# Attention with a gated MLP on one core: four score banks that also hold the maxima's first-block scores and the values' output

## Chip, core and metric

The kernel runs on one core of a Trainium2 chip. The metric is device time in microseconds (us), the median of three runs: 740.32 us before the change (739.99 to 740.38). The profiled execution, from which all durations are taken, took 740.08 us.

## What is computed

The input x has 2048 tokens of 512 channels. It is normalized; one branch is attention with 32 heads of 16 channels in which each token sees itself and the 255 tokens before it, the other is an MLP with 1792 hidden channels whose result, through SiLU, gates the first.

```
xn = layernorm(x)
q, k, v = heads of (xn @ wqkv)                       # 32 heads x 16
scores = q k^T / 4, kept where 0 <= i - j < 256
s = (softmax(scores) @ v) @ wo
g = silu(gelu(layernorm(xn) @ w1 + b1) @ w2 + b2)
out = x + s * g
```

All is float32. The matmuls work on pairs of rounded parts: each operand is split into a high part and the rest, and three products (high x high, high x rest, rest x high) are summed.

## The kernel before

**The slots.** Attention runs over 8 groups of four heads (n) and 16 blocks of 128 keys (kb); one slot t = 16 n + kb handles one key block of one group. A loop (line 834) writes the slots' instructions out in order, and the class Ordered (line 27) keeps each engine to the order in which the code names them, so the order on TensorE is that of this loop. Within a slot stand, in order:

1. `prob_block(.., 1)` (line 555): the scores of head pair 1. Two matmuls (one for each head, in the two halves of the array's rows) give 128 keys x up to 384 queries into two PSUM banks; ScalarE takes the exponential of both into SBUF (tile pt), and GpSimd sets to zero what lies outside the window.
2. `max_block` (line 503) for the query block 12 slots ahead (LEAD): four matmuls give the scores of that block against its own and the preceding key block in xy (two banks). VectorE copies into the masked places the scores against the first key block of the window (`first_scores`, line 494; four matmuls into zo), by a predicated copy, and reduces the maxima over keys. These maxima go back into the operands later, so that the exponentials need no further subtraction. Query blocks 0 and 1 of a group have no first block and take a constant.
3. `fill_in(t, 0)`: a share of other work for TensorE, cut into small units: projections of later groups, later the values' projection and MLP products. `tandem` (line 440) spreads two such jobs over several slots, with a high half and a low half of the contraction in the two halves of the array's rows, into the two banks fb; its function `places` (line 449) says how many units go to the first half of a slot and how many to the second. When a tandem ends (slot t1) both banks are copied out, by ScalarE in most of them.
4. `prob_block(.., 0)`: the scores of head pair 0.
5. `fill_in(t, 1)`: the second share of other work.
6. `first_scores` for the next slot's query block, both pairs.
7. `pv_step` (line 577): the values of the slot before: for up to three key blocks and four heads a matmul of 17 x 128 into otb, four of them side by side in the array's columns. ScalarE (VectorE in the slots where a tandem has just ended) copies otb to oraw.

**Where these lie in PSUM.** There are eight banks of 512 columns. xy has two. zo has two: columns 0 to 256 of both hold the first-block scores, columns 256 to 384 of the second hold the values' output otb (line 195). fb has two, for fills. The last two are a pool of single banks (ps_st) before slot 0, for transposes and the first values' projections, and from slot 0 on the tile stb, the scores of a pair; both pairs of a slot use it in turn. In the last 12 slots, which have no maxima left, pair 1 uses xy instead.

**After the slots** comes the MLP with the gated output, in another set of PSUM tiles. The change does not touch it.

## Time and profile before

| | before |
|---|---|
| median of runs | 740.32 us |
| profiled execution | 740.08 us |
| its span | 738.4 us |
| TensorE busy | 725.1 us (98%) |
| VectorE busy | 509.8 us (69%) |
| ScalarE busy | 444.0 us (60%) |
| GpSimd busy | 297.6 us (40%) |
| granted TensorE clock, mean | 0.999 |

How to read the profile: the span runs from the first to the last instruction. PE is the matmuls of TensorE, PEld its weight loads, DVE is VectorE, ACT ScalarE, POOL GpSimd, SP the engine that issues DMAs. Matmuls are pipelined and their ends are modelled, so neighbouring rows can overlap a little. In the timeline a row is a run of like instructions: start, length, engine, line, operation, output <- inputs, shapes, count, and in brackets the idle time before it with what ended it. In the groups by shape the columns are the group and its count, then busy time and mean ns of one, then the idle time ahead of them, by what ended it. All instructions carry line 43, that of the helper that issues them, so groups are told apart by the names of tiles: pt<-stb is an exponential, stb<-qk the scores of a pair, xy<-qk the maxima's scores, zo<-qk the first-block scores, zo<-pt,vt the values, fb fills, oraw<-zo the copy of the values' output, xy<-upper,zo the predicated copy.

### The profile page before, as it was taken

How to read it: one execution, taken by the hardware profiler on the slowest of the kernel's cores; microseconds unless marked ns; L12 is line 12 of the kernel's file. 1: busy time of each engine (PE TensorE's matmuls, PEld its weight loads, DVE VectorE, ACT ScalarE, POOL GpSimd, SP SyncE). 2: the span in 40 equal slices, each digit the busy share in tenths (PEclk: the TensorE clock that was granted, in tenths of full speed). 3: DMA queues.
4: the chain of work that ended last, by engine and by line, in shares of the span. 5: the costliest groups of instructions: out<-in, count | busy, mean ns of one | idle time of the engine just before them, and what ended most of it. 6: DMA issues, size and time to landing. Idle time of an engine off the chain costs nothing.

```text
span 738.4 us, 18757 instructions
## 1 busy us (share of the span) xinstructions
PE 725.1 (98%) x7360; PEld 587.2 (80%) x7360; DVE 509.8 (69%) x790; ACT 444.0 (60%) x744; POOL 297.6 (40%) x644
## 2 busy tenths in 40 slices
PE   8999999999999999999999999999999999999997
PEld 7886777777778888777776688888888888888886
DVE  7886677877766678887772577656667855667733
ACT  7757767877777676778877756443644734541001
POOL 7413757867666555767867600120102000001102
PEclk9999999999999999999999999999999999999999
DMA  8633356766555524747724397657452322163711
GB/s 292 194 69 77 83 144 165 198 162 186 146 145 148 158 66 153 177 127 184 206 84 148 106 323 194 178 134 206 108 110 100 111 76 86 60 183 118 228 40 57
DMA packets 84697, 105.71 MB, mean 143 GB/s; under 512 B 37312, under 2 KB 37568, under 8 KB 84608
## 3 DMA queue, kind: packets, MB, share of 16 engines
q1 hardware_dynamic: 84608, 104.51, 50.7%
q8 instruction: 58, 0.95, 0.5%
q14 instruction: 31, 0.25, 0.1%
HBM read 54.53 MB, written 32.77 MB: 118 GB/s over the span
## 4 chain that ended last, share of the span: by engine, by line
PE 91%; ACT 4%; DVE 2%; POOL 1%; DMA 1%; issue 1%; SPq 0%; DVEq 0%; ACTq 0%
PE acc L43 21%; PE fb L43 19%; PE zo L43 13%; PE stb L43 9%; PE p L43 9%; PE s L43 6%; PE h L43 6%; PE xy L43 5%; ACT pt L43 4%; PE pv L43 3%; POOL pt L43 1%; DVE xy L43 1%; DMA x<-in_x_dram 1%; DVE mt L43 0%; PE tr L43 0%
## 5 line engine op out<-in xcount | busy, mean ns | idle before, releaser
L43 POOL TENSOR_SCALAR_AFFINE_SELECT pt<-pt 128x256 f32<-128x256 f32 x480 | 193.0, 426 | 128.9 <-ACT pt L43 126.1
L43 ACT ACTIVATE pt<-stb 128x768 f32<-128x768 f32 (+1 forms) x244 | 188.7, 773 | 52.6 <-PE stb L43 46.3
L43 DVE TENSOR_REDUCE mt<-xy 128x4 f32<-128x1024 f32 (+1 forms) x128 | 152.6, 1192 | 4.4
L43 DVE COPY_PREDICATED xy<-upper,zo 128x512 f32<-128x512 int32 x112 | 77.8, 694 | 70.4 <-PE xy L43 63.0
L43 POOL TENSOR_TENSOR xo<-xo,gated 128x512 f32<-128x512 f32 x15 | 19.9, 1328 | 235.0 <-DVE gated L43 195.6
L43 PE MATMUL fb<-xnT,wqb 64*128 64x512 f32 (+1 forms) x684 | 104.6, 397 | 0.0
L43 PE MATMUL zo<-pt,vt 128*17 128x128 f32 x2880 | 103.7, 275 | 0.3 <-POOL pt L43 0.3
L43 PE MATMUL stb<-qk 64*128 64x384 f32 (+1 forms) x488 | 94.6, 383 | 6.0 <-ACT pt L43 4.3
L43 PE MATMUL acc<-w,gh 128*128 128x512 f32 x320 | 98.4, 389 | 0.0
L43 PEld LDWEIGHTS stb<-qk 64*128 64x128 f32 x488 | 45.8, 183 | 48.3 <-ACT pt L43 41.4
L43 PEld LDWEIGHTS zo<-pt,vt 128*17 128x17 f32 x2880 | 67.5, 97 | 15.6 <-issue 5.0
L43 PEld LDWEIGHTS fb<-xnT,wqb 64*128 64x128 f32 (+1 forms) x684 | 64.8, 185 | 9.5 <-issue 0.6
L43 PEld LDWEIGHTS acc<-w,gh 128*128 128x128 f32 x320 | 60.1, 188 | 12.4
L43 PE MATMUL acc<-w,gl 128*128 128x512 f32 x160 | 62.2, 389 | 0.0
L43 PE MATMUL xy<-qk 64*128 64x256 f32 (+2 forms) x536 | 58.3, 291 | 0.2 <-DVE mt L43 0.2
L43 PEld LDWEIGHTS xy<-qk 64*128 64x128 f32 x536 | 46.6, 185 | 6.8 <-issue 3.2
L43 ACT COPY oraw<-zo 128x128 f32<-128x128 f32 x108 | 28.7, 266 | 30.8 <-PE zo L43 20.4
L43 ACT ACTIVATE gated<-acc 128x512 f32<-128x512 f32 x16 | 8.7, 595 | 59.3 <-DVE acc L43 59.3
L43 PE MATMUL s<-wos,ohl 128*128 128x512 f32 (+1 forms) x204 | 44.3, 376 | 0.0
L43 PEld LDWEIGHTS s<-wos,ohl 128*128 128x128 f32 x204 | 36.8, 188 | 7.1
L43 ACT COPY p<-p 128x512 f32<-128x512 f32 x21 | 12.3, 585 | 48.6 <-PE p L43 41.4
L43 PEld LDWEIGHTS zo<-qk 64*128 64x128 f32 x448 | 37.5, 185 | 4.8 <-DVE xy L43 1.8
(190 smaller groups left out, 1238.9 us busy)
## 6 DMA issues: line engine op xcount, KB each, us to landing
qk<-sh SPq DMA_DIRECT2D x128, 128.0 KB
qk<-pjr SPq DMA_DIRECT2D x64, 128.0 KB
oT_d<-oraw SPq DMA_DIRECT2D x32, 256.0 KB
w_d<-in_w_dram SPq DMA_DIRECT2D x14, 512.0 KB
x<-in_x_dram SPq DMA_DIRECT2D x16, 256.0 KB
or<-oT_d SPq DMA_DIRECT2D x16, 256.0 KB
w<-rden_d SPq DMA_DIRECT2D x16, 256.0 KB
xo<-in_x_dram SPq DMA_DIRECT2D x16, 256.0 KB
```

What stands on the lines that cost most here:

```text
L43: r = issue(*args, **kwargs)
```

## The change

The scores get a tile of four banks, `four`, indexed by head pair, head and column: pair p uses `four[:, p]` in every slot, columns 0 to 384. Its last 128 columns in each of the four banks hold the first-block scores of the maxima (one bank for each pair and head), and in the last bank (pair 1, head 1) also the values' output otb, in the same 128 columns at another time of the slot. zo is now a name for the two banks of pair 1, and the pool of single banks of the early phase becomes the two banks of pair 0 in turn (`early_bank`). xy and fb stay.

The order in a slot changes with it. The first-block scores of pair 1 are issued in `max_block`, in the slot itself, behind the maxima's scores. Those of pair 0 are issued a slot ahead, directly behind the scores of pair 0 and ahead of `fill_in(t, 1)`. In `places`, a slot of a tandem leaves at least n/12 of its units to the second half, so that a fill stands between them and the values. The copy of a tandem's second bank moves from the second to the first half of slot t1.

```diff
@@ -191,19 +191,22 @@
     xy = psum.tile([P, 2, 512], F32, name="xy")
-    zo = psum.tile([P, 2, 512], F32, name="zo")
-    otb = zo[:, 1, 256:384]
+    four = psum.tile([P, 2, 2, 512], F32, name="four")
+    zo = four[:, 1]
+    otb = four[:, 1, 1, 384:512]
...
-    early = ExitStack()
-    ps_st = early.enter_context(tc.tile_pool(name="ps_st", bufs=2, space=PSUM))
-    stb = []
-    turn = [1]
+    turn, swap = [1], [1]
...
+    def early_bank():
+
+        swap[0] ^= 1
+        return four[:, 0, swap[0]]
@@ -452,7 +455,7 @@
-                ahead = min(b - a, 5 * n // 12) if t < 16 * NQ - LEAD else min(b - a, max(most, (b - a + 1) // 2))
+                ahead = min(b - a - n // 12, 5 * n // 12) if t < 16 * NQ - LEAD else min(b - a, max(most, (b - a + 1) // 2))
@@ -475,7 +478,7 @@
-        fills.setdefault((t1, 1), []).append((two[2], (fb[1], t1, copy)))
+        fills[t1, 0].append((two[2], (fb[1], t1, copy)))
@@ -491,13 +494,19 @@
-    def first_scores(n, qb):
-
-        slot = slots[n % 2]
-        for p in range(2):
+    def first_place(n, qb):
+
+        if 16 * n + qb < LEAD:
+            return zo[:, :, 0:256].rearrange("q a (p k) -> q p a k", p=2)
+        return four[:, :, :, 384:512]
+
+    def first_scores(n, qb, ps=range(2)):
+
+        slot, place = slots[n % 2], first_place(n, qb)
+        for p in ps:
             for a in (1, 0):
                 r = slice(64 * a, 64 * a + 64)
-                nc.tensor.matmul(zo[:, a, P * p: P * (p + 1)], slot[r, 0, p, P * qb: P * (qb + 1)],
+                nc.tensor.matmul(place[:, p, a], slot[r, 0, p, P * qb: P * (qb + 1)],
                                  slot[r, 1, p, P * (qb - 2): P * (qb - 1)], start=True, stop=True)
@@ -512,13 +521,13 @@
-        if qb >= 2 and not ahead:
-            first_scores(n, qb)
+        if qb >= 2:
+            first_scores(n, qb, (1,) if ahead else range(2))
...
-                                  neg if qb < 2 else zo[:, :, 0:256].rearrange("q a (p k) -> q a p k", p=2))
+                                  neg if qb < 2 else first_place(n, qb).rearrange("q p a k -> q a p k"))
@@ -556,7 +565,7 @@
-        both = xy if p and 16 * n + kb + LEAD >= 16 * NQ else stb[0]
+        both = four[:, p]
@@ -852,11 +857,11 @@
             prob_block(t // 16, t % 16, 0)
+        if t >= 0 and m + 1 < end and (m + 1) % 16 >= 2 and m + 1 not in IN_PLACE:
+            first_scores((m + 1) // 16, (m + 1) % 16, (0,))
         fill_in(t, 1)
         if 0 <= m < 4:
             max_block(0, m)
-        if t >= 0 and m + 1 < end and (m + 1) % 16 >= 2 and m + 1 not in IN_PLACE:
-            first_scores((m + 1) // 16, (m + 1) % 16)
         if t >= 1:
             pv_step((t - 1) // 16, (t - 1) % 16)
```

More of the change, by code (lines that the diff above doesn't have):

```diff
@@ L247, in mm @@
                 box.append([fb[0], fb[1], zo[:, 0], None][kt] if c == 1 and kt < 3 else fill_bank() if c > 1 and kt in (1, 2) else
-                           ps_st.tile([P, 512], F32, tag="b", name=f"tr_{c}_{kt}"))
+                           early_bank())
             nc.tensor.transpose(box[kt][:, P * i: P * (i + 1)], xs[c][i][:, P * kt: P * (kt + 1)], ident)
@@ L352, in mm @@
             if k == 0:
-                box.append(ps_st.tile([P, 2, 256], F32, tag="b", name=f"pv_{hf}_{i}"))
+                box.append(early_bank().rearrange("p (j t) -> p j t", j=2))
             j, kt, (a, b) = k // 12, k % 12 // 3, PASSES[k % 3]
@@ L514, in max_block @@
                                  slot[r, 1, p, P * lo: P * (qb + 1)], start=True, stop=True)
-        if qb >= 2 and not ahead:
-            first_scores(n, qb)
-        four = xy.rearrange("q a (p k) -> q a p k", p=2)
-        nc.vector.copy_predicated(four[:, :, :, 128:256], mask,
-                                  neg if qb < 2 else zo[:, :, 0:256].rearrange("q a (p k) -> q a p k", p=2))
+        if qb >= 2:
+            first_scores(n, qb, (1,) if ahead else range(2))
+        parts = xy.rearrange("q a (p k) -> q a p k", p=2)
+        nc.vector.copy_predicated(parts[:, :, :, 128:256], mask,
+                                  neg if qb < 2 else first_place(n, qb).rearrange("q p a k -> q a p k"))
         nc.vector.tensor_reduce(out=mts[n, qb // 4][:, :, :, qb % 4],
-                                in_=four[:, :, :, off:256],
+                                in_=parts[:, :, :, off:256],
                                 axis=AX.X, op=ALU.max, negate=True)
@@ L698, in mixer_kernel @@
             nc.sync.dma_start(xs[c][i], x[512 * c + P * i: 512 * c + P * (i + 1), :])
-    tr0 = [ps_st.tile([P, 512], F32, tag="b", name=f"tr_0_{kt}") for kt in range(2)] + fb
+    tr0 = [early_bank() for _ in range(2)] + fb
     def transpose0(i):
@@ L840, in mixer_kernel @@
         if 0 <= t < end:
-            if t == 0:
-                early.close()
-                stb.append(attn.enter_context(tc.tile_pool(name="ps_s2", bufs=1, space=PSUM)).tile(
-                    [P, 2, 512], F32, name="stb"))
             prob_block(t // 16, t % 16, 1)
```

## Prediction

> **What bounds the kernel now.** I read the page first: engine shares and the chain that ended last.

> ```profile
> span 738.4 us, 18757 instructions
> PE 725.1 (98%) x7360; PEld 587.2 (80%) x7360; DVE 509.8 (69%) x790; ACT 444.0 (60%) x744; POOL 297.6 (40%) x644
> PE 91%; ACT 4%; DVE 2%; POOL 1%; DMA 1%; issue 1%; SPq 0%; DVEq 0%; ACTq 0%
> ```

> TensorE (PE) is busy for 98% of the span and is 91% of the chain. ScalarE (ACT), the next on the chain, has 4%. So a change can save little except matmul work, and anything that makes TensorE wait goes straight into the time. Next the windows over the attention slots (columns: length, PE, PEld, DVE, ACT, POOL busy, granted clock, DMA):

> ```profile
> 0.00:5.00 5.00, 3.71 (x17) 3.71 (x18) 3.02 (x8) 4.03 (x2) 4.01 (x10) 1.00 0.58 187
> ...
> 100.00:200.00 100.00, 98.27 (x1515) 77.13 (x1513) 73.56 (x92) 75.70 (x130) 68.66 (x160) 1.00 0.65 169
> 300.00:400.00 100.00, 97.60 (x1480) 74.43 (x1482) 74.27 (x98) 79.48 (x137) 75.30 (x168) 1.00 0.58 161
> ```

> Where the slots run, PE is busy 98% and ScalarE and VectorE (DVE) only some 75%. Then the timeline of PE alone, and of ScalarE alone, over one slot:

> ```profile
> 304.45 0.85 PE L43 MATMUL zo<-pt,vt 128*17 128x128 f32 x24
> 305.72 0.44 PE L43 MATMUL stb<-qk 64*128 64x384 f32 x2 [0.41 <-ACT pt L43]
> 306.00 0.40 PE L43 MATMUL xy<-qk 64*128 64x256 f32 x4
> 306.23 1.16 PE L43 MATMUL fb<-xnT,wqb 64*128 64x512 f32 x8
> 307.22 0.35 PE L43 MATMUL stb<-qk 64*128 64x384 f32 x2
> 307.39 0.35 PE L43 MATMUL zo<-qk 64*128 64x128 f32 x4
> 307.67 0.85 PE L43 MATMUL zo<-pt,vt 128*17 128x128 f32 x24
> 308.47 0.44 PE L43 MATMUL stb<-qk 64*128 64x384 f32 x2
> ```

> ```profile
> 304.85 0.82 ACT L43 ACTIVATE pt<-stb 128x768 f32<-128x768 f32 x1
> 305.55 0.59 ACT L43 COPY pjr<-fb 128x512 f32<-128x512 f32 x1
> 306.20 0.81 ACT L43 ACTIVATE pt<-stb 128x768 f32<-128x768 f32 x1
> 306.91 0.61 ACT L43 CAST sh<-pjr 128x512 fp32r<-128x512 f32 x1
> 307.61 0.81 ACT L43 ACTIVATE pt<-stb 128x768 f32<-128x768 f32 x1
> 308.63 0.27 ACT L43 COPY oraw<-zo 128x128 f32<-128x128 f32 x1 [0.21 <-PE zo L43]
> ```

> A slot from one score pair to the next takes 308.47 - 305.72 = 2.75 us, and PE fills it: scores of pair 1 (0.28), four maxima products (0.23), eight fill products (0.99), scores of pair 0 (0.17), four first-block products (0.28), the values (0.80). Both exponentials (0.81 each) and the copy of the values' output (0.27) run beside that. PE waits for ScalarE only when the next score pair wants the one score buffer (0.41 at 305.72: ScalarE's exponential ended at 305.67).

> These rows price a wait. From the start of a score pair to its exponential: 306.20 - 305.72 = 0.48 after a wait, 307.61 - 307.22 = 0.39 behind other matmuls. From the exponential's end to the matmul that waited: 305.72 - 305.67 = 0.05. From the values' start to their copy's start: 308.63 - 307.67 = 0.96. One fill product: 0.99/8 = 0.12.

> **Does a wait go by columns or by bank?** This decides the case, since the new places share banks. In the kernel before, the first-block scores lie in columns 0 to 256 of the two zo banks, the values' output in columns 256 to 384 of the second: no column in common. By shape:

> ```profile
> L43 DVE COPY_PREDICATED xy<-upper,zo 128x512 f32<-128x512 int32 x112 | 77.8, 694 | 70.4 <-PE xy L43 63.0 <-PE zo L43 5.6 <-ACT oraw L43 0.8
> L43 PEld LDWEIGHTS zo<-pt,vt 128*17 128x17 f32 x2880 | 67.5, 97 | 15.6 <-issue 5.0 <-DVE xy L43 1.4 <-ACT pt L43 0.7
> ```

> VectorE's copy, which reads the scores, waited for ScalarE's copy of the output (ACT oraw, 0.8 us in all), and the values' weight loads waited for VectorE's copy (DVE xy, 1.4). So waits go by bank. [...]

> The changed program's order on TensorE, with waits, for one steady slot (four = the new tile):

> ```
> four<-qk_91 128x384 [waits DMAHW7_49,Activation_49]   scores, pair 1
> xy<-qk_91 128x256 [waits DVE_49]                      maxima
> four<-qk_91 128x128 [waits Activation_49]             first block, pair 1
> fb_108<-xnT,wqb_2237 128x512 ...                      fill
> four<-qk_91 128x384 [waits DVE_49]                    scores, pair 0
> four<-qk_91 128x128 [waits Activation_49]             first block, next head block, pair 0
> ```

> Each wait's count names its producer: the copy of the slot before's output (first), this slot's own exponential of pair 1 (third), VectorE's predicated copy (fifth), and this slot's own exponential of pair 0 (last). TensorE takes instructions in this order, so all behind a waiting one (fills, values, the next slot) waits too.

> **The change part by part.** No matmul, exponential or copy is added or removed; 2.75 us of PE work a slot stays.

> *A, scores of pair 1 behind the copy of the output.* The copy now sits between the values and the next scores: 0.96 + 0.27 + 0.05 = 1.28 from the values' start. Before, that distance is 0.80 (307.67 to 308.47), 1.27 at 304.45, and on average 0.83 over the 105 full groups (x24) followed by scores, the first and the last of which are:

> ```profile
> 73.36 0.85 PE L43 MATMUL zo<-pt,vt 128*17 128x128 f32 x24
> 74.34 0.44 PE L43 MATMUL stb<-qk 64*128 64x384 f32 x2
> ...
> 418.50 0.85 PE L43 MATMUL zo<-pt,vt 128*17 128x128 f32 x24
> 419.28 0.33 PE L43 MATMUL xy<-qk 64*128 64x128 f32 x2
> ```

> +0.45 in 126 slots is 57 us (0.31 to 0.48: 39 to 60). The old stall for the single score buffer is inside this difference.

> *C, first block of pair 1 behind the exponential of pair 1.* From the score pair's start: 0.48 + 0.81 + 0.05 = 1.34. PE has only the maxima products as cover and would go on at 306.23 - 305.72 = 0.51. +0.83, in 102 slots (0 to 115, without the 14 whose query block is 0 or 1): 85 us. Two slots in 16 have narrower exponentials:

> ```profile
> L43 ACT ACTIVATE pt<-stb 128x768 f32<-128x768 f32 x214 | 173.9, 813 | 47.6 <-PE stb L43 41.5 <-ACT qk L43 0.5
> L43 ACT ACTIVATE pt<-stb 128x512 f32<-128x512 f32 x15 | 9.0, 599 | 3.0 <-PE stb L43 3.0
> L43 ACT ACTIVATE pt<-stb 128x256 f32<-128x256 f32 x15 | 5.8, 385 | 2.0 <-PE stb L43 1.8
> ```

> That takes 7 x (0.21 + 0.43) = 4.5 off: 80.

> *F, first block of pair 0 behind the exponential of pair 0.* It stands directly behind its scores, with no cover at all; the fill meant for this half comes after it. 0.44 (between 0.39 and 0.48) + 0.81 + 0.05 = 1.30, where PE went on after 0.17: +1.13 in 100 slots, less 4.5 for the narrow ones: 108 us.

> *E, scores of pair 0 behind the predicated copy.* How long after its products the copy starts:

> ```profile
> 114.68 0.40 PE L43 MATMUL xy<-qk 64*128 64x256 f32 x4
> ...
> 115.18 0.70 DVE L43 COPY_PREDICATED xy<-upper,zo 128x512 f32<-128x512 int32 x1 [0.77 <-PE xy L43]
> ```

> 0.50 from the start of four products, so some 0.38 from the start of the two of pair 1; copy 0.69, restart 0.05: 1.12. Cover: 0.14 for the two products to issue, and fills. Six fills (0.73) leave 0.25, eight or more nothing. Some 60 slots have six: 15 us (0 if the fills cover it; 27 if the copy, which now reads four banks in place of two, is slower by 0.2; the trace of before has no such copy).

> *P, both fill banks' copies ahead of pair 0's exponential* where a tandem ends (the second stood behind it before). The fills end about 2.5 us into the slot (1.34 + 0.14 + 0.73 and the last product's length); 2 x 0.59 from there push the exponential from 2.9 (1.34 + 1.12 + 0.44) to 3.7: 0.8 in the 16 such slots with F, 13 us (0 to 20).

> *At nothing:* the early phase swaps two pool banks for the same two in turn, with PE's order kept (0, or a few us either way); the fill moved to just before the values is issued either way; the xy buffer freed in the last 12 slots only leaves A.

> Sum: 57 + 80 + 108 + 15 + 13 = 273. The profiled execution took 740.08 (span 738.4 and 1.7 around it), 0.24 under the median of 740.32. 740.08 + 273 = 1013 us. Slots go from 2.80 (127 between the first and last values)

> ```profile
> 67.98 0.41 PE L43 MATMUL zo<-pt,vt 128*17 128x128 f32 x8
> ...
> 424.07 0.85 PE L43 MATMUL zo<-pt,vt 128*17 128x128 f32 x24
> ```

> to about 4.9.

> **Rivals.** *Waits by columns (faster).* If the first-block scores wait only for whoever touches their own columns, C, E and F vanish, A shrinks, and doubled score buffers remove PE's idle ahead of the scores:

> ```profile
> L43 PE MATMUL stb<-qk 64*128 64x384 f32 x428 | 85.5, 395 | 6.0 <-ACT pt L43 4.3
> ```

> 740.1 - 6.0 = 734 us. It decides if the third and last wait above count to an earlier ScalarE instruction than the slot's own exponential. For: nothing but disjoint columns; against: the two by-shape rows and the counts. 4%.

> *TensorE's clock falls.* The new slot leaves PE idle for some 2 of its 4.9 us, in three gaps of up to 1.1. If the granted clock were halved through the slots, 2.80 us of work would double: up to 127 x 2.80 = 356 more, towards 1,370; a part of the time, 1,100 to 1,200. Against: 1.00 in the window 0 to 5, where PE is busy 3.71 of 5 us. [...] No row here has a half-idle PE. 7%.

> *ScalarE's queue becomes the bound.* ScalarE has 1.9 us a slot of exponentials and output (2 x 0.81 + 0.27), and casts and copies of 0.6 (305.55, 306.91). If each of the 56 casts and copies of the projections stood before an exponential that PE awaits, 56 x 0.6 = 34 more, 13 of it counted: 1030, with the upper ends of A, E and P 1060 to 1090. Against: C to F leave ScalarE over 1 us between its exponentials. 8%.

> That the time stays within 0.2% (about what a measurement of this kernel tells from no change) needs A to F to cancel: 1%.

> **How the numbers follow.** Forecast 80%: 1013. Low end (0.39 from each score pair to its exponential): A 39, C 75, F 104, E 0, P 5: 963. High end (0.48, nothing off for the narrow ones in C): A 60, C 85, F 113, E 27, P 20, half of ScalarE's 34: 1062. 963 to 1062 holds the forecast case and half of ScalarE's; the clock and columns stay outside. Faster 0.04, same 0.01, slower 0.95.

> **What would show it.** In the changed profile: TensorE's share falls to about 72% (725 of 1013); waits of the first-block products on ACT pt near 180 us in all, of the scores on the output's copy near 60; a full slot near 5 us; ScalarE's and VectorE's busy time unchanged; all after the slots shifted, not changed. The prediction is wrong if the first-block products start before their slot's exponential has ended, or if the granted clock leaves 1.00.

## The result and the profile after

The changed kernel takes 1277.95 us (median of four runs, 1271.06 to 1290.36) against 740.22 us before: 1.7234 times as long (95% interval 1.7141 to 1.7327). That ratio leaves out the longest of the four runs, which counts as a slow one. The profiled execution took 1281.77 us. The range ended at 1062.

The page of the changed kernel, as far as it answers the lines shown of before (behind each engine's name the busy time and its share of the span; in the row PEclk the mean granted clock, in tenths, in 40 equal slices of the span; in the last row the shares of the chain that ended last):

```profile
span 1280.1 us, 18874 instructions
...
PE 1032.5 (81%) x7360; PEld 735.3 (57%) x7360; DVE 508.5 (40%) x790; ACT 448.2 (35%) x744; POOL 294.0 (23%) x644
...
PEclk8986555656555566575556555655679999999999
...
PE 75%; ACT 18%; issue 3%; DVE 3%; ACTq 0%; DMA 0%; DVEq 0%; POOL 0%
```

The same 7360 matmuls take 1032.5 us in place of 725.1, and the clock row says why: from the fourth slice to the end of the slots, 96 to some 965 us, TensorE was granted 5 to 7 tenths of its clock in the mean of a slice. VectorE, ScalarE and GpSimd are as busy as before in microseconds. The window over the slots, of the changed kernel:

```profile
100.00:400.00 300.00, 223.39 (x1813) 139.44 (x1815) 86.54 (x108) 93.52 (x156) 85.06 (x201) 0.56 0.25 62
```

and of the kernel before:

```profile
100.00:400.00 300.00, 293.88 (x4668) 233.80 (x4668) 221.17 (x282) 226.38 (x385) 205.79 (x480) 1.00 0.58 155
```

In 300 us 1813 matmuls instead of 4668, at a clock of 0.56 instead of 1.00. One slot of the changed kernel, TensorE alone:

```profile
499.94 0.69 PE L43 MATMUL four<-qk 64*128 64x384 f32 x2 [0.47 <-DVE oraw L43]
500.42 0.63 PE L43 MATMUL xy<-qk 64*128 64x256 f32 x4
501.53 0.47 PE L43 MATMUL four<-qk 64*128 64x128 f32 x2 [0.48 <-ACT pt L43]
501.80 2.44 PE L43 MATMUL fb<-wva,xnT 64*128 64x256 f32 x20
504.04 0.53 PE L43 MATMUL four<-qk 64*128 64x384 f32 x2
505.47 0.47 PE L43 MATMUL four<-qk 64*128 64x128 f32 x2 [0.90 <-ACT pt L43]
505.74 0.74 PE L43 MATMUL fb<-wva,xnT 64*128 64x256 f32 x4
506.41 1.48 PE L43 MATMUL four<-pt,vt 128*17 128x128 f32 x24
508.36 0.69 PE L43 MATMUL four<-qk 64*128 64x384 f32 x2 [0.47 <-ACT oraw L43]
```

A, C and F stand in the brackets, in their places: 0.47 behind the output's copy, 0.48 behind the exponential of pair 1, 0.90 behind that of pair 0. But the matmuls between them are long: the values take 1.48 where they took 0.85, a score pair 0.69 where it took 0.44. In the last slots, where the clock is back, the same 24 products read 0.85 again (same kernel):

```profile
958.07 1.48 PE L43 MATMUL four<-pt,vt 128*17 128x128 f32 x24
...
962.04 0.85 PE L43 MATMUL four<-pt,vt 128*17 128x128 f32 x24 [0.90 <-ACT pt L43]
```

Where the 541.7 us of the span (1280.1 - 738.4) lie is read from the first and the last values group. Before they start at 67.98 and 424.07. The changed kernel:

```profile
101.89 0.63 PE L43 MATMUL four<-pt,vt 128*17 128x128 f32 x8
...
965.77 0.85 PE L43 MATMUL four<-pt,vt 128*17 128x128 f32 x24
```

33.9 us are lost before the first values, 507.8 between first and last (6.80 us for each of 127 intervals, 2.80 before), nothing after (314.3 us both times).

### The profile page after: what moved, and what is told of

The parts are those of the page before. It is cut to its first block, busy times and chain, and to the rows that moved or that the text cites. A ratio compares the mean times of both kernels' runs of the same rounds, so it can differ in the third digit from the quotient of the medians.

```text
span 1280.1 us, 18874 instructions
## 1 busy us (share of the span) xinstructions
PE 1032.5 (81%) x7360; PEld 735.3 (57%) x7360; DVE 508.5 (40%) x790; ACT 448.2 (35%) x744; POOL 294.0 (23%) x644
## 4 chain that ended last, share of the span: by engine, by line
PE 75%; ACT 18%; issue 3%; DVE 3%; ACTq 0%; DMA 0%; DVEq 0%; POOL 0%
PE four L43 32%; PE fb L43 18%; ACT pt L43 14%; PE acc L43 12%; PE p L43 5%; PE s L43 3%; PE h L43 3%; ACT oraw L43 2%; PE xy L43 1%; DVE xy L43 1%; ACT pjr L43 1%; DVE xnT L43 1%; DVE mt L43 0%; DVE oraw L43 0%; ACT vt L43 0%
## 5 line engine op out<-in xcount | busy, mean ns | idle before, releaser
L43 PE MATMUL four<-qk 64*128 64x128 f32 (+1 forms) x960 | 238.0, 497 | 205.2 <-ACT pt L43 144.9
L43 POOL TENSOR_SCALAR_AFFINE_SELECT pt<-pt 128x256 f32<-128x256 f32 x480 | 187.9, 414 | 658.2 <-ACT pt L43 658.0
L43 PEld LDWEIGHTS four<-qk 64*128 64x128 f32 x960 | 129.6, 268 | 361.2 <-ACT pt L43 227.3
L43 ACT ACTIVATE pt<-four 128x768 f32<-128x768 f32 (+2 forms) x256 | 197.7, 772 | 331.8 <-PE four L43 321.5
L43 DVE COPY_PREDICATED xy<-upper,four 128x512 f32<-128x512 int32 x112 | 78.0, 696 | 491.7 <-PE four L43 458.4
L43 PE MATMUL fb<-xnT,wqb 64*128 64x512 f32 (+1 forms) x684 | 185.1, 622 | 0.0
L43 PE MATMUL four<-pt,vt 128*17 128x128 f32 x2880 | 163.0, 384 | 19.1 <-ACT pt L43 19.0
L43 DVE TENSOR_REDUCE mt<-xy 128x4 f32<-128x1024 f32 (+1 forms) x128 | 152.6, 1192 | 4.4
L43 PEld LDWEIGHTS four<-pt,vt 128*17 128x17 f32 x2880 | 92.0, 128 | 81.5 <-ACT pt L43 32.6
L43 PEld LDWEIGHTS fb<-xnT,wqb 64*128 64x128 f32 (+1 forms) x684 | 102.8, 304 | 12.7
L43 ACT COPY oraw<-four 128x128 f32<-128x128 f32 x108 | 28.7, 266 | 225.4 <-PE four L43 224.4
L43 PE MATMUL acc<-w,gh 128*128 128x512 f32 x320 | 98.6, 389 | 0.0
L43 PE MATMUL xy<-qk 64*128 64x256 f32 (+1 forms) x512 | 75.0, 387 | 0.0
L43 POOL TENSOR_TENSOR xo<-xo,gated 128x512 f32<-128x512 f32 x15 | 20.0, 1331 | 234.9 <-DVE gated L43 233.0
L43 PEld LDWEIGHTS xy<-qk 64*128 64x128 f32 x512 | 71.4, 293 | 3.2 <-issue 1.9
L43 PEld LDWEIGHTS acc<-w,gh 128*128 128x128 f32 x320 | 60.1, 188 | 12.5
L43 PE MATMUL acc<-w,gl 128*128 128x512 f32 x160 | 62.2, 389 | 0.0
L43 PE MATMUL fb<-wva,xnT 64*128 64x256 f32 x384 | 47.5, 399 | 0.0
L43 PE MATMUL fb<-xnT 64*128 64x512 f32 (+1 forms) x176 | 45.2, 558 | 0.0
L43 PE MATMUL s<-wos,ohl 128*128 128x512 f32 (+1 forms) x204 | 44.3, 376 | 0.0
L43 PEld LDWEIGHTS fb<-wva,xnT 64*128 64x128 f32 x384 | 41.1, 297 | 0.0
L43 PEld LDWEIGHTS s<-wos,ohl 128*128 128x128 f32 x204 | 36.8, 188 | 7.1
```

The costliest lines, as they stand in the source:

```text
L43: r = issue(*args, **kwargs)
```

## The experiments

Two theories were set against each other. **Waits and clock:** the waits cost what was forecast, and the rest is the granted clock, which falls because TensorE idles. **Waits alone:** the waits are longer than priced, and the low clock costs nothing, since TensorE waits anyway. The times of e1 to e6 and e8 to e12 are of one profiled execution each, beside 739.79 to 740.41 of the kernel before.

### More work in the gaps: e1, e4, e8

The maxima products write their result to xy anew each time, so they can be issued again without changing anything but TensorE's time. e4 issues them twice (in `max_block`), e8 four times, e1 four times and once more ahead of the scores of pair 1.

```diff
 def max_block(n, qb, ahead=False):
-        for p in range(2):
+        for p in [0, 1] * (4 if 16 * n + qb >= LEAD else 1):     # e4: 2
...
+        if t >= 0 and m < end:                                    # e1 only
+            products(m // 16, m % 16)
         if 0 <= t < end:
             prob_block(t // 16, t % 16, 1)
```

> The changed kernel with TensorE's maxima products repeated (the same result written again): once ahead of the scores of pair 1, where TensorE waits for the copy of the output, and four times in place of once behind them, where it waits for the exponential. 16 matmuls more in each of 116 slots. Theory 'waits and clock': the waits alone cost what was forecast (about 273 us in the slots, 34 more before them) and the rest of the 540 us is the granted clock, which falls because TensorE idles; filling the gaps A and C brings the clock up, and the kernel gets FASTER with more work: below 1200 us, towards 1050 if the clock comes back to 1.0. Rival 'waits alone': the waits are longer than forecast, the low clock costs nothing because TensorE waits anyway; more work can't help: 1280 or more.

> The changed kernel with the maxima products of each slot issued twice in place of once (four matmuls more a slot, some 0.25 us of the 0.83 us gap at C). 'Waits and clock': the clock rises a little from the 0.55 that it has in the slots, and the time falls by less than in the run with more repeats, to between 1200 and 1275. 'Waits alone': 1280, nothing or a little more.

> As e1, without the repeat ahead of the scores of pair 1 (in e1 the copy of the output started only after those products, so that A grew). The gap C alone is filled, 12 matmuls more in each of 116 slots. 'Waits and clock': the waits at full clock, corrected for what the traces have shown (273 forecast, 34 before slot 0, some 30 for the values that wait for the exponential of pair 0 in the 27 slots without a first block), make 1077 us; with the clock at 0.9 to 1.0 the time is 1065 to 1120. If the clock stays under 0.8, as in e4, it is 1150 to 1200.

e4 took 1202.58 us, e8 1135.93, e1 1109.38: with 4, 12 and 16 matmuls **more** in each of 116 slots the kernel is 79, 146 and 172 us faster than its 1281.77. The same window in e4, then e8, then e1:

```profile
100.00:400.00 300.00, 222.55 (x2231) 144.72 (x2231) 99.58 (x123) 104.23 (x175) 95.22 (x220) 0.77 0.30 74
```

```profile
100.00:400.00 300.00, 226.77 (x2783) 161.57 (x2781) 104.70 (x130) 110.81 (x186) 102.17 (x237) 0.91 0.30 75
```

```profile
100.00:400.00 300.00, 245.50 (x3173) 171.98 (x3177) 109.91 (x136) 116.31 (x194) 106.60 (x249) 0.98 0.32 79
```

The clock goes 0.56, 0.77, 0.91, 0.98 as the gaps fill. "Waits alone" is refuted: it allowed no gain. e4 came out at the low end of its range, e8 above the 1120 that a clock of 0.9 to 1.0 should have given, e1 above the hoped-for 1050. In e1 the copy of the output started only behind the products put ahead of it:

```profile
501.37 0.85 PE L43 MATMUL four<-pt,vt 128*17 128x128 f32 x24
502.15 0.50 PE L43 MATMUL xy<-qk 64*128 64x256 f32 x4
503.01 0.44 PE L43 MATMUL four<-qk 64*128 64x384 f32 x2 [0.36 <-ACT oraw L43]
```

From the values to the next scores 1.64 us, 0.36 more than A was priced at, so up to 42 us of e1 are its own.

### Waits by tile: e2

The four banks are one tile. e2 gives the phase before slot 0 its own tiles again and opens the four-bank tile at slot 0.

```diff
-    four = psum.tile([P, 2, 2, 512], F32, name="four")
-    zo = four[:, 1]
-    otb = four[:, 1, 1, 384:512]
+    early = ExitStack()
+    ps_zo = early.enter_context(tc.tile_pool(name="ps_zo", bufs=1, space=PSUM))
+    zo = ps_zo.tile([P, 2, 512], F32, name="zo")
+    ps_st = early.enter_context(tc.tile_pool(name="ps_st", bufs=2, space=PSUM))
...
     def early_bank():
-        swap[0] ^= 1
-        return four[:, 0, swap[0]]
+        return ps_st.tile([P, 512], F32, tag="b", name="eb")
...
+        if t == 0:
+            early.close()
+            four = attn.enter_context(tc.tile_pool(name="ps_four", bufs=1, space=PSUM)).tile(
+                [P, 2, 2, 512], F32, name="four")
+            otb = four[:, 1, 1, 384:512]
+            nc.vector.memset(otb, 0.0)
```

> The changed kernel with tiles of their own for the phase before slot 0 (a tile of two banks for the first-block scores and a pool of two single banks, as before), closed at slot 0, where the four-bank tile is opened. If waits go by tile (any access of another engine to any bank of one tile holds up TensorE's next write to that tile), the phase before slot 0 loses its 27 us: some 1250 us. If waits go by bank, as the prediction had it, that phase waits as it did: 1280 us, slot 0 again at 89 us and not at 62.

It took 1261.28 us. The total says little, since four runs of the changed kernel lie 19 us apart. The first values say it (e2):

```profile
75.78 0.63 PE L43 MATMUL four<-pt,vt 128*17 128x128 f32 x8
```

75.78 instead of 101.89: 26.1 of the 33.9 us lost before the first values come from the one tile. The scores of slot 0 start at 63.33 in e2, 61.92 before and 89.19 in the changed kernel; the other 7.8 us lie mostly in slots 0 and 1, ahead of the first values. In the changed kernel that phase shows what waited:

```profile
39.39 0.66 PE L43 MATMUL four<-ident,x 128*128 128x128 f32 x4 [0.53 <-DVE xnT L43]
39.98 0.50 PE L43 MATMUL xy<-qk 64*128 64x256 f32 x4
40.72 0.44 PE L43 MATMUL four<-qk 64*128 64x128 f32 x4 [0.24 <-ACT xnT L43]
44.47 4.62 PE L43 MATMUL four<-wva,xnT 128*128 128x256 f32 x24 [3.31 <-DVE xnT L43]
```

Transposes into one bank wait for VectorE reading the other (0.53 us); first-block scores in the banks of pair 1 wait for ScalarE reading a bank of pair 0 (0.24 us). So the program's waits go by tile, across its banks.

### Without the waits, one after the other: e3, e5, e6, e9, e10

e3 issues the first-block scores of each pair ahead of that pair's scores, in the four-bank tile. e5 keeps the changed kernel's order but has one tile of two banks for each pair (and e2's early tiles), with the predicated copy in two. e6 is e5 with e3's order. e9 is e6 with C put back, e10 is e6 with F put back.

```diff
+        if t >= 0 and m < end and m % 16 >= 2:                     # e3, e6, e10
+            first_scores(m // 16, m % 16, range(2) if m in IN_PLACE else (1,))
         if 0 <= t < end:
             prob_block(t // 16, t % 16, 1)
...
+        if t >= 0 and m + 1 < end and (m + 1) % 16 >= 2 and m + 1 not in IN_PLACE:   # e3, e6, e9
+            first_scores((m + 1) // 16, (m + 1) % 16, (0,))
         if 0 <= t < end:
             prob_block(t // 16, t % 16, 0)
...
+            four = [ps_four.tile([P, 2, 512], F32, name=f"four{p}") for p in range(2)]   # e5, e6, e9, e10
...
+            for p in range(2):
+                nc.vector.copy_predicated(parts[:, :, p, 128:256], mask1, first_place(n, qb, p))
```

> The changed kernel with the first-block scores issued ahead of the scores of their pair and not behind them: the waits C and F for the slot's own exponentials are gone, A (the copy of the output) and a longer E (the predicated copy, which still comes behind the exponential of pair 1) stay. At a full clock a slot would take 1.28 + 2.2 + 0.6 = 4.1 us, 940 us in all with the loss before slot 0. 'Waits and clock': TensorE still idles some 1.2 us of 4.1, so the clock stays below 1.0 and the time is above that, 950 to 1170. 'Waits alone': the share of C and F in the 508 us that the slots lost (188 of 273) goes: 930.

> The changed kernel's banks and order, but one tile of two banks for each pair in place of one of four (and tiles of their own before slot 0), and the predicated copy in two, one for each pair's tile. 'Waits and clock', with waits by tile: the loss before slot 0 goes (20 us, as in e2), the values no longer wait for the exponential of pair 0 in the slots without a first block, and the scores of pair 0 wait only for their own half of the predicated copy; A, C and F are within one bank and stay, so TensorE still idles over 2 us a slot and the clock stays under 0.7: 1180 to 1250 us. If A, C and F also come from the one tile alone, they go, and the time is under 800.

> As e5, with the first-block scores ahead of the scores of their pair, as in e3. Only A is left of the waits (0.45 us a slot), with at most 0.2 us before the values for pair 1's half of the predicated copy. 'Waits and clock': idle under 0.7 us of 3.3 in each slot; with the clock near 1.0 the time is 740 + 127 x (0.45 to 0.65) = 797 to 823 us. 'Waits alone', in which the forecast waits were too short by the ratio 508 to 273: 850 to 900, at whatever clock.

> e6 (tiles by pair, only A left, 810 us) with the first-block scores of pair 1 back behind the scores of pair 1: C alone is added. The prediction's price of C at full clock is 80 us: 890 if the clock holds. TensorE then idles 1.3 us of 4.0 a slot (a third), more than in e3 (clock 0.78 to 0.90), so 'waits and clock' expects a granted clock of 0.6 to 0.9 in the slots and 920 to 1050 us; 'waits alone' 880 to 900.

> e6 with the first-block scores of pair 0 back behind the scores of pair 0: F alone is added. Price of F at full clock 108 us: 918 if the clock holds. Idle 1.6 us of 4.2 a slot: 'waits and clock' expects a granted clock of 0.55 to 0.85 in the slots and 960 to 1080 us; 'waits alone' 905 to 930.

| run | waits left (P aside) | us | clock, 100 to 400 us |
|---|---|---|---|
| changed | A, C, E, F, values | 1281.8 | 0.56 |
| e5 | A, C, F | 1183.8 | 0.61 |
| e3 | A, E, values | 1050.7 | 0.80 |
| e10 | A, F | 1048.8 | 0.65 |
| e9 | A, C | 891.1 | 1.00 |
| e6 | A | 809.6 | 1.00 |

e6 falls in the middle of its range. Its slots take (492.60 - 71.09)/127 = 3.32 us from the first to the last values, 0.51 more than before, where A was priced at 0.45; the row of A (e6):

```profile
302.27 0.85 PE L43 MATMUL four<-pt,vt 128*17 128x128 f32 x24
303.55 0.55 PE L43 MATMUL four<-qk 64*128 64x128 f32 x4 [0.43 <-ACT oraw L43]
```

1.28 from values to what waits for their copy (here the first-block scores), as worked out. e9 adds C: 891.1 - 809.6 = 81.5 us, priced at 80, and 3.0 of them lie before the first values (74.14 against 71.09). Its clock was misjudged, it stayed at 1.00 in the window, and so its time lies in the range of "waits alone" and not in that of "waits and clock". e10 adds F: 239.2 us for a wait priced at 108, with the clock at 0.65. e3, e5 and e10 lie in the ranges of "waits and clock"; "waits alone" gave 930 for e3 and 905 to 930 for e10. In e3 the values still share one tile with the exponential of pair 0, in other banks ("values" in the table; 19.0 us of that wait read in the changed kernel, below), so e3 is not as far from the changed kernel as was meant; in e10, which has a tile for each pair like e5, e6 and e9, two rows of values from 105 us on wait for an exponential, 0.73 and 0.74 us. e5's 1184 keeps A, C and F, whose two sides share a bank, as expected; that they came from the four-bank tile alone is out. No run puts two tiles into one bank, so whether they go by the bank or by the two-bank tile is not shown.

### Share or length of the gaps: e11, e12

e11 is e9 and e12 is e10 with the maxima products issued four times, the edit of e8.

> e9 with the maxima products issued four times in place of once (same result, 12 matmuls more a slot), so that TensorE works through the gap at C. 'Waits and clock': the granted clock is back at 0.95 or more and the time is that of e6 plus the price of C at full clock, 885 to 910 us, less than e9 although there is more work. 'Waits alone': no less than e9.

> e10 with the maxima products issued four times in place of once. There is no gap at C in e10, so the 12 matmuls more a slot stand on TensorE's own time (some 0.83 us at full clock, 96 us in 116 slots), and the gap F behind the scores of pair 0 stays exactly as long as it was. If the granted clock follows the share of time in which TensorE is busy, that share rises from about 69% (at full clock) to about 75%, the clock comes back to 0.9 or more, and the kernel takes 1010 to 1045 us, less than e10 (1049) with more work on the path. If the clock follows the length of the longest gap, it stays at 0.65 as in e10, and the time is 1150 to 1210 us.

e11 took 901.4 us, 10 more than e9: the time fits, but as e9's clock was whole, there was nothing to win, and "less than e9" was wrong, as "waits alone" had it. e12 took 1034.45, 14 less than e10, though its repeats stand on TensorE's own time. The 14 us alone are less than the 19 by which runs of the changed kernel differ; but the case of the longest gap asked for 1150 to 1210. The window of e10, then of e12:

```profile
100.00:400.00 300.00, 232.90 (x2340) 157.75 (x2328) 114.82 (x181) 113.30 (x190) 101.47 (x240) 0.65 0.31 79
```

```profile
100.00:400.00 300.00, 227.53 (x3178) 171.41 (x3176) 122.19 (x193) 119.80 (x201) 109.11 (x254) 0.95 0.33 84
```

In e12 the gap F is as long as it was (0.91 in brackets, like e10's):

```profile
303.36 0.44 PE L43 MATMUL four<-qk 64*128 64x384 f32 x2
304.71 0.33 PE L43 MATMUL four<-qk 64*128 64x128 f32 x2 [0.91 <-ACT pt L43]
```

The clock is 0.95 and not 0.65, with the same gap of 0.91 us. So in these two runs the longest gap alone doesn't set the clock; what goes with it is how much of the time TensorE works, seen in short windows.

```profile
262.46:265.88 3.42, 3.00 (x34) 1.71 (x32) 2.11 (x4) 1.85 (x4) 1.38 (x4) 0.50 0.02 5
265.88:269.29 3.41, 2.97 (x48) 2.23 (x48) 1.56 (x3) 2.43 (x5) 2.77 (x7) 1.00 0.17 36
...
282.94:286.35 3.41, 2.35 (x38) 1.37 (x34) 2.17 (x4) 1.85 (x4) 2.72 (x5) 1.00 0.36 76
286.35:289.77 3.42, 1.81 (x16) 1.19 (x16) 2.08 (x3) 2.66 (x5) 0.76 (x2) 1.00 0.55 118
289.77:293.18 3.41, 2.78 (x32) 2.03 (x34) 0.29 (x1) 0.16 (x1) 0.77 (x2) 0.50 0.44 128
```

Behind the stretch with 1.81 us of work the clock halves; behind the one with 3.00 it is whole again. Counted from the first to the last values of all fourteen traces (before, changed, e1 to e12): TensorE worked for under 0.62 of the time in 161 of the 168 full-clock stretches behind which the clock halved, and in 102 of the 1441 behind which it stayed. From half clock it came back behind 174 stretches, all with at least 0.82, and behind none of the 543 with less. A gap of 0.8 to 1.0 us was the longest in 92 full-clock stretches with a fall behind them and in 254 without one.

### Can the banks be had without the waits: e7

e7 is e6 with the second share of fills behind the values, two units in most slots, so that the output's copy runs beside them.

```diff
-                ahead = min(b - a - n // 12, 5 * n // 12) if t < 16 * NQ - LEAD else ...
+                ahead = min(b - a - n // 6, 5 * n // 12) if t < 16 * NQ - LEAD else ...
...
         if t >= 1:
             pv_step((t - 1) // 16, (t - 1) % 16)
+        if t >= 0:
+            fill_in(t, 1)
```

> As e6, with the second share of fills behind the values (two units at least in most slots), so that the copy of the output runs beside them and A is covered; the last slot of a tandem's first phase keeps its units ahead. Both theories: no wait of the changed kernel is left, the clock is 1.0, and the time is that of the kernel before within 10 us (730 to 750), with a small gain if the doubled score banks remove TensorE's 6 us of waits ahead of the scores, a small loss if the two halves of the predicated copy and the values' wait for pair 1's half cost more.

789.35 us, 1.0665 times before (1.0647 to 1.0683): A is in part covered (a slot takes 0.37 us more than before, 0.51 in e6), and the time is not within 10 us of before. Its waits on TensorE's weight loads (engine, what waited, for whom: us in total, times, longest):

```profile
PEld four L43 <- DVE xy L43: 51.8, 160, 0.7
...
PEld four L43 <- ACT oraw L43: 33.6, 91, 1.0
...
PEld four L43 <- DVE oraw L43: 17.6, 20, 1.1
```

The values now wait for pair 1's half of the predicated copy, and the output's copy still shows where a slot has no fill behind its values. No version here beats the kernel before.

## Why the prediction was wrong

**Where the waits stand** was right. The first-block scores wait for their own slot's exponentials, the scores for the output's copy; columns that differ don't help. The rival "waits by columns" is out: within one tile, nothing went by columns.

**What they cost at full clock** was about right. A: 0.51 us a slot against 0.45, measured in e6. C: 81.5 us against 80, in e9 less e6. F: 304.71 - 303.36 = 1.35 from the scores to the first block in e12, against 1.30. P was not measured by itself. E looks small: TensorE's matmuls read 3.6 us of waits in all for the predicated copy in the changed kernel, 4.3 in e1, where 15 were forecast. e1, at a clock of 0.98, bounds the sum: its values lie 793.20 - 101.64 = 691.6 us apart, 335 more than the 356.1 of before, of which up to 42 are its own; so 293 to 335, where 273 were forecast, and some 20 of these are a wait that the sum lacked (below).

**"At nothing: the early phase"** failed. The first scores of slot 0, before and then in the changed kernel:

```profile
61.92 0.44 PE L43 MATMUL stb<-qk 64*128 64x384 f32 x2
```

```profile
89.19 0.44 PE L43 MATMUL four<-qk 64*128 64x384 f32 x2
```

27.3 us later. The step said "two pool banks for the same two in turn", and "waits go by bank". The program's waits go by tile, and the change made one tile out of banks that had been three tiles. The two rows quoted for the bank rule could not have shown it: zo was one tile as well as shared banks. The same rule of the tile makes the values wait for the exponential of pair 0 in the slots without a first block, a term that the sum lacked, as the group of the values in the changed kernel shows (idle time ahead of it):

```profile
L43 PE MATMUL four<-pt,vt 128*17 128x128 f32 x2880 | 163.0, 384 | 19.1 <-ACT pt L43 19.0
```

**The sum was made at full clock**, and this is the step that failed by most: the prediction left the lower clock out of its range. Its own sign of being wrong, that the granted clock leaves 1.00, came true. The rival that had it right got 7%. Against it stood a window of 5 us with 3.71 us of work and a clock of 1.00; what gaps of up to 1.1 us do to the clock was shown by no row of before. In the changed kernel 206 of the 226 waits of matmuls for an exponential are no longer than that (us in total, times, longest):

```profile
PE four L43 <- ACT pt L43: 163.9, 226, 1.7
...
PE four L43 <- ACT oraw L43: 49.0, 106, 0.5
```

The clock is 0.56 all the same, and e12, at 0.95 with the gap F of e10, shows that the longest gap alone doesn't decide. Between the first and the last values of the changed kernel the clock goes back and forth between half and full: it halved 12 times and came back 13 times. The prediction had also named 180 us of waits of the first-block products on the exponentials, and 60 of the scores on the output's copy. By shape they are 142.5 and 50.5 (42.5 for ScalarE's copy, 8.0 for VectorE's): the places were right, the sizes somewhat too high. Idle time in a row counts from the modelled end of the matmul ahead, and reads less than a wait costs: in e9, at the full clock, the waits of C read 62.4 us where C cost 81.5. At half clock longer matmuls reach into it as well (the gap at C reads 0.48 in the slot shown, 0.67 in a slot of e9). The window of 5 us with a clock of 1.00 proved nothing: the first clock record in the trace of before starts 7.08 us into the span, and the view shows 1.00 where there is none. Between the first and the last values the clock is half for 86% of the time, and the 1,278 us lie between the rival's two prices, 1,100 to 1,200 for part of the time and 1,370 throughout.

The clock's part is estimated as what the slots lost beyond the waits that e1 shows: 507.8 less 335 or 293, that is 173 to 215 us. Of the 541.7 us that is 32 to 40%; the waits, with that of the values, are 54 to 62%; the one tile before the slots makes 26 us.

What stays open: why the clock stayed whole behind 102 full-clock stretches with under 0.62 of work, and why it came back behind some of the half-clock stretches with 0.82 or more and not behind 252 others. The share of work is what TensorE's rows show, whose ends are modelled.

## What to carry to other kernels

The waits on TensorE cost twice here: first their own length, then slower matmuls around them (24 products of the values in 1.48 us and not 0.85). When a change leaves TensorE idle for a good part of each slot, though in short gaps, price the low clock as a likely case: in these runs 161 of the 168 falls came behind stretches of 3.41 us with under 0.62 of work. Expect it to stay, too: it came back behind none of the 543 half-clock stretches with less than 0.82, and in the changed kernel 204 of the 217 half-clock stretches were followed by another. And to see whether it is at work, add harmless matmuls in the gaps: with 16 more a slot the changed kernel was 172 us faster, its clock 0.98 and not 0.56 (e1). Put into one PSUM tile only what may wait for each other: the one tile cost 26.1 us before the slots (e2).

## Of the hardware, not expected

- With gaps mostly of 0.4 to 1.0 us in the slots of the changed kernel (6.80 us each on average), no wait of a matmul for an exponential over 1.7, the granted clock was 0.56 on average; the same 24 products took 1.48 us at the low clock and 0.85 at the full one.
- The fall is graded only in the mean: 0.56, 0.77, 0.91 and 0.98 with 0, 4, 12 and 16 products added a slot. In the clock records it reads 1.00 or 0.50; from the first to the last values it is half for 86, 53, 17 and 7% of the time.
- The share of work over a long window doesn't tell the clock in these runs, as the matmuls are longer at the low clock (1.48 us and 0.85, above): TensorE worked for 227.28 us of 300 in e9 (window 100 to 400) at 1.00, for 226.77 in e8 at 0.91 and for 232.90 in e10 at 0.65.
